# Weight conversion stores half a step earlier, a fourth float64 buffer, and 512-token x tiles in an attention and two-MoE kernel

## The chip, the cores and the metric

The kernel runs on one core of a Trainium2 chip. The metric is the device time of one execution in microseconds (us), lower is better; what is given for a kernel is the median of its runs.

## The reference

The input is attention over 4 batches of 8 heads, 576 positions, 64 dimensions per head, with a mask in blocks of 64, followed by two feed-forward layers ("MoE" in the names, with one expert each). All arithmetic is wanted at float32 accuracy; the weights arrive as float64.

```python
def _attn_ref(q, k, v):                       # 4 x 8 x 576 x 64
    scores = np.matmul(q, k.transpose(0, 1, 3, 2)) / np.sqrt(D)
    scores = np.where(pos[:, None] // 64 >= pos[None, :] // 64, scores, -1e9)
    attn = np.exp(scores - scores.max(-1, keepdims=True))
    attn = attn / (attn.sum(-1, keepdims=True) + 1e-09)
    return np.matmul(attn, v)

x = attn_out.transpose(0, 2, 1, 3).reshape(2304, 512)
h = x @ moe_w_in                              # 512 -> 2048
x = np.maximum(0.01 * h, h) @ moe_w_out       # 2048 -> 512
h = x @ moe2_w_in
P = a[0] + a[1] * h + a[2] * h**2 + a[3] * h**3
Q = 1.0 + abs(b[0]) * abs(h) + abs(b[1]) * h**2
out = (P / (Q + 1e-6)) @ moe2_w_out           # 2304 x 512
```

## The kernel before

Nearly every product is computed as three TensorE matmuls over a high and a low part of each operand (`xh`, `xl` for the attention output x; `wh`, `wl` for the weights). The program has three stretches.

**Attention** goes over 32 heads (`n`, batch `b = n // 8`). The steps of a head are letters in a string (`ORDER`): "1" splits q and k of the next head and loads a later one (L230, L231), "v" splits v and loads the next pair of heads, "x", "y", "z" are scores, maximum and exponential (L294, L300, L306), "a" and "b" the transposes and their split (L343, L328, L336), and "4" is `apply(n - 2)`, the product with v (`a4`, L371 and L375). At its end `a4` writes x. For the first eight heads ("whole") it is taken from PSUM by ACT and DVE (L382, L383). For the others ACT copies one half of the PSUM tile into `xs` (L385), DVE adds the other half (L386), and after every second head ACT and POOL split `xs`, which holds the 128 rows of two heads, into `xh` and `xl` (L388, L389). `xs` is part of the tile `vr`.

**The weight conversion** (`convert`, 64 blocks of 128x512 weights) runs between those steps. A block is loaded into `cs` as pairs of 32-bit words (L146, 512 KB). ACT changes the high word (L164), POOL (first 16 blocks) or ACT the low word (L168, L170), DVE joins the two into a float32 in `cl` (L179), ACT rounds its high part into `ch`, or for the first layer into the resident `w1i`, `w1o` (L182), and POOL subtracts it in place, which leaves the low part in `cl` (L183). The parts are stored to device memory by `write_block` (L153): 256 KB per block for the first 32 blocks (the low part only), twice 256 KB for the last 32, which are the second layer's weights. `cs` and `cl` have three buffers each, `ch` two. `convert` is a generator that yields twice per block. In the first half of a step it issues the load of block i+1 and the work of ACT and POOL on block i; in the second half the join, rounding and subtraction of block i-1, and then the stores of block i-2. A table of due times (`due`, `pace`) says how many halves have been issued after each attention step.

**The first feed-forward layer** (`moe1`) is the filler: from the second batch on `fill` puts some of its matmuls (L446) behind each attention step. Its work is cut into units of 12 matmuls, 32 units per batch of 512 tokens. A unit needs one tile of low weights, `wl`, which is read back from device memory (L418, 256 KB): `wl` has four buffers, and unit u, after its first matmul, issues the load for unit u+3. The 64 tokens per batch beyond 512 are stored to `xld` (`save_left`, L426, two stores of 128 KB per batch, of the high and the low part) and read back into the tile `xleft`, which makes a fifth group of 256 tokens and 32 units after the fourth batch. After the attention, `moe1` runs alone, and then **the second layer** (`moe2`, L548 to L602) follows.

The tiles `xh` and `xl` are 4x576 floats wide, of which `moe1` reads 4x512 directly.

What sets the order: the DMA queue of SP (every load and store of the kernel) is issued in the order of the program text, and SP waits at an instruction whose data or buffer is not ready. The instructions of the other engines are placed by a scheduler.

Of the kernel before, what the change touches and what calls it, by code (L numbers as in the profile page):

```python
# [25 lines left out]
def attention_moe_moe_kernel(  # L26
# [41 lines left out]
    xld = [dram.tile([P, KD, B, NL], F32, name=f"xld{i}") for i in range(2)]  # L68
# [34 lines left out]
    acc = w1.tile([P, KD, NT1], F32, name="acc")  # L103
    pTw = acc.rearrange("p k n -> p (k n)")
# [38 lines left out]
    def load_block(i):  # L143
        if i < len(blocks):
            stage[i] = cp.tile([P, 512, 2], I32, tag="cs", name="cs", bufs=3)
            nc.sync.dma_start(out=stage[i].rearrange("p (r n) w -> p r (n w)", r=KD), in_=blocks[i][0])  # L146
# [9 lines left out]
    def convert():  # L156
        load_block(0)
        load_block(1)
        for i in range(len(blocks) + 1):
            if i > 0:  # L160
                load_block(i + 1)
# [9 lines left out]
            if i > 0:  # L171
# [12 lines left out]
                write_block()  # L184
# [175 lines left out]
    def a4(n):  # L360
# [20 lines left out]
        if whole:  # L381
            nc.scalar.copy(xh[r, j, :], T[r, 384:960])  # L382
            nc.vector.tensor_tensor(xl[r, j, :], T[r, 384:960], xh[r, j, :].bitcast(F32), ALU.subtract)  # L383
# [3 lines left out]
        if e == 1:  # L387
            nc.scalar.copy(xh[:, j, :], xs)  # L388
            (nc.vector if h == H - 1 else nc.gpsimd).tensor_tensor(xl[:, j, :], xs, xh[:, j, :].bitcast(F32), ALU.subtract)  # L389

    X = {}

# [11 lines left out]
    wt = {}  # L404
    prepped = [0]

    def prep_w1(u):
        while prepped[0] <= min(u, len(units) - 1):
# [8 lines left out]
            wl = mp.tile([P, 4, P], F32R, tag="wl", name="wl", bufs=4)  # L417
# [5 lines left out]

    def save_left(b):
        for t, x in zip(xld, X[b]):
            nc.sync.dma_start(out=t[:, :, b, :], in_=x[:, :, NT1:S].bitcast(F32))  # L426

    def moe1(g):
        xh, xl = X[g]
        n = NT1 if g < B else B * NL  # L430
        for u in range(g * NU, (g + 1) * NU):
# [13 lines left out]
            for m, (w, kk, lo) in enumerate(seq):  # L445
                nc.tensor.matmul(T, lhsT=w[:, kk, :], rhs=A[kk][lo], start=(m == 0), stop=(m == 11))  # L446
                yield
                if m == 0:
                    prep_w1(u + 3)
# [56 lines left out]
    def x_tiles():  # L506
        return tuple(xp.tile([P, KD, S], F32R, tag=nm, name=nm) for nm in ("xh", "xl"))
# [128 lines left out]
    with tc.manual_schedule(engines={mybir.EngineType.SP}):  # L636
# [50 lines left out]
        for n, (b, h) in enumerate(heads):  # L687
# [8 lines left out]
            for step, f in zip(steps, fills):  # L696
# [9 lines left out]
                elif step == "4":  # L706
                    apply(n - 2)
# [20 lines left out]
            if h == 1 and b > 0:  # L728
                save_left(b - 1)
# [3 lines left out]
        apply(NHD - 1)  # L733
        att.close()
        xq.append(ctx.enter_context(tc.tile_pool(name="xq0", bufs=1, side="right", reuse_waits="tile")))
        w2a = ctx.enter_context(tc.tile_pool(name="w2a", bufs=1, side="right", reuse_waits="tile"))
        X[B] = tuple(w2a.tile([P, KD, B * NL], F32R, name=f"xleft{i}") for i in range(2))
# [3 lines left out]
        for i in range(32):  # L741
            fill(24)
            if i == 1:
                save_left(B - 1)
                for t, x in zip(X[B], xld):
                    nc.sync.dma_start(out=t.bitcast(F32), in_=x.rearrange("p k b t -> p k (b t)"))
# [53 lines left out]
```

## Time and profile before

| what | us |
|---|---|
| median of 3 runs | 1052.45 (1050.78 to 1053.03) |
| the profiled execution, its own time | 1051.65 |
| span of its trace | 1049.8 |
| TensorE matmul busy | 1001.1 (95%) |
| VectorE (DVE) busy | 725.7 (69%) |
| ScalarE (ACT) busy | 664.8 (63%) |
| GpSimd (POOL) busy | 297.4 (28%) |

The profile is of one execution. The difference between its time and the span, 1.85 us, lies outside the trace. The attention lasts to about 500 us (the last L385 starts at 499.4), the filler starts at about 85 us, the four full groups of the first layer end at about 597.8, the left-over group at about 646.6, and the second layer takes the rest. Engines are named as in the rows: PE is TensorE's matmuls, PEld its weight loads, SPq the queue on which SP issues DMAs. `L446 <- DVE vr L386` means that an instruction of line 446 waited for the DVE instruction of line 386 that writes `vr`.

### The profile page before, as it was taken

How to read it: one execution, taken by the hardware profiler on the slowest of the kernel's cores; microseconds unless marked ns; L12 is line 12 of the kernel's file. 1: busy time of each engine (PE TensorE's matmuls, PEld its weight loads, DVE VectorE, ACT ScalarE, POOL GpSimd, SP SyncE). 2: the span in 40 equal slices, each digit the busy share in tenths (PEclk: the TensorE clock that was granted, in tenths of full speed). 3: DMA queues.
4: the chain of work that ended last, by engine and by line, in shares of the span. 5: the costliest groups of instructions: out<-in, count | busy, mean ns of one | idle time of the engine just before them, and what ended most of it. 6: DMA issues, size and time to landing. Idle time of an engine off the chain costs nothing.

```text
span 1049.8 us, 14585 instructions
## 1 busy us (share of the span) xinstructions
PE 1001.1 (95%) x4968; PEld 826.8 (79%) x4968; DVE 725.7 (69%) x1232; ACT 664.8 (63%) x1355; POOL 297.4 (28%) x369
## 2 busy tenths in 40 slices
PE   6978888998999999999999999999999999999998
PEld 4757767777888878878888898888888888888886
DVE  3676767776667677775222223999888888888875
ACT  5766777867677776775311223876766666676675
POOL 4787646755454654543100101000000000000000
PEclk9999999999999999999999999999999999999999
DMA  7467768668666686564665588802102010110010
GB/s 195 148 179 244 223 203 269 204 211 275 202 190 210 220 275 196 190 211 121 226 205 197 188 278 295 327 1 81 41 1 81 1 40 1 41 41 1 1 41 21
DMA packets 104105, 159.36 MB, mean 152 GB/s; under 512 B 13152, under 2 KB 50016, under 8 KB 104032
## 3 DMA queue, kind: packets, MB, share of 16 engines
q1 hardware_dynamic: 104032, 158.44, 47.0%
q8 instruction: 39, 0.64, 0.3%
q14 instruction: 34, 0.28, 0.1%
HBM read 117.44 MB, written 40.37 MB: 150 GB/s over the span
## 4 chain that ended last, share of the span: by engine, by line
PE 60%; DMA 11%; DVE 9%; ACT 7%; POOL 6%; issue 4%; SPq 3%; POOLq 0%; DVEq 0%; ACTq 0%
PE h L548 19%; PE o L602 19%; PE M L446 18%; DMA cs<-in_moe_w_out_dram 4%; POOL PB L316 3%; DMA cs<-in_moe_w_in_dram 2%; ACT PB L306 2%; DVE cl L179 2%; PE T L343 1%; DVE pTl L336 1%; DMA w1l<-cl 1%; DVE nm L300 1%; DMA wl<-w1l 1%; POOL cl L183 1%; DMA w2l<-cl 1%
## 5 line engine op out<-in xcount | busy, mean ns | idle before, releaser
L446 PE MATMUL M<-gh,w1o 128*128 128x512 f32 (+1 forms) x320 | 120.3, 377 | 5.2 <-DVE vr L386 4.7
L446 PE MATMUL M<-gh,wl 128*128 128x512 f32 (+1 forms) x320 | 119.8, 375 | 0.3 <-DMA wl<-w1l 0.3
L446 PE MATMUL M<-gl,w1o 128*128 128x512 f32 (+1 forms) x320 | 120.0, 376 | 0.0
L316 POOL TENSOR_SCALAR PB<-PB,sm 128x448 f32<-128x448 f32 (+4 forms) x160 | 95.1, 616 | 65.4 <-DVE sm L313 61.4
L560 ACT ACTIVATE ea<-h,coef 128x512 f32<-128x512 f32 (+1 forms) x80 | 51.7, 646 | 93.5 <-PE h L548 93.5
L306 ACT ACTIVATE PB<-T,nm 128x448 f32<-128x448 f32 (+4 forms) x160 | 83.0, 524 | 35.7 <-DVE nm L300 29.0
L455 DVE TENSOR_TENSOR gl<-M,gh 128x512 fp32r<-128x512 f32 (+1 forms) x80 | 50.4, 633 | 79.1 <-ACT M L454 78.8
L453 ACT ACTIVATE gh<-M 128x512 fp32r<-128x512 f32 (+1 forms) x80 | 44.4, 555 | 93.4 <-PE M L446 93.2
L548 PE MATMUL h<-x2h,w2h 128*128 128x512 f32 (+1 forms) x240 | 89.0, 371 | 0.5 <-DVE acc L462 0.5
L548 PE MATMUL h<-x2h,w2l 128*128 128x512 f32 (+1 forms) x240 | 88.9, 370 | 0.0
L548 PE MATMUL h<-x2l,w2h 128*128 128x512 f32 (+1 forms) x240 | 88.8, 370 | 0.0
L602 PE MATMUL o<-w2h,g2l 128*128 128x512 f32 x216 | 84.7, 392 | 0.0
L602 PE MATMUL o<-w2h,g2h 128*128 128x512 f32 x216 | 84.7, 392 | 0.0
L602 PE MATMUL o<-w2l,g2h 128*128 128x512 f32 x216 | 84.6, 391 | 0.0
L343 PE MATMUL T<-ident,PB 128*128 128x128 f32 x480 | 68.9, 282 | 15.9 <-POOL PB L316 8.5
L300 DVE TENSOR_REDUCE nm<-T 128x1 f32<-128x448 f32 (+4 forms) x160 | 70.9, 479 | 15.6 <-PE T L288 9.9
L563 DVE SCALAR_TENSOR_TENSOR ea<-eh,coef,ea 128x512 f32<-128x512 f32 (+1 forms) x80 | 55.6, 696 | 35.7 <-ACT eh L561 35.2
L343 PEld LDWEIGHTS T<-ident,PB 128*128 128x128 f32 x480 | 56.2, 144 | 30.5 <-POOL PB L316 12.0
L179 DVE SCALAR_TENSOR_TENSOR cl<-cs 128x512 int32<-128x512 int32 x64 | 55.0, 859 | 36.4 <-DMA w2l<-cl 10.6
L446 PE MATMUL M<-xh,w1i 128*128 128x512 f32 x256 | 75.6, 404 | 3.8 <-DVE vr L386 3.2
L446 PE MATMUL M<-xh,wl 128*128 128x512 f32 x256 | 74.7, 408 | 0.0
L446 PE MATMUL M<-xl,w1i 128*128 128x512 f32 x256 | 72.6, 397 | 2.1 <-DVE xl L383 1.1
(117 smaller groups left out, 2504.3 us busy)
## 6 DMA issues: line engine op xcount, KB each, us to landing
wl<-w1l SPq DMA_DIRECT2D x160, 256.0 KB, 3.2
cs<-in_moe_w_in_dram SPq DMA_DIRECT2D x32, 512.0 KB, 5.0
cs<-in_moe_w_out_dram SPq DMA_DIRECT2D x32, 512.0 KB, 5.3
w1l<-cl SPq DMA_DIRECT2D x32, 256.0 KB, 4.7
w2h<-ch SPq DMA_DIRECT2D x32, 256.0 KB, 3.8
w2l<-cl SPq DMA_DIRECT2D x32, 256.0 KB, 3.9
w2h<-w2h SPq DMA_DIRECT2D x12, 512.0 KB, 7.0
w2l<-w2l SPq DMA_DIRECT2D x12, 512.0 KB, 7.7
```

Source lines behind the costliest of these rows:

```text
L179: nc.vector.scalar_tensor_tensor(f.bitcast(I32), hi, 3, lo, ALU.logical_shift_left, ALU.bitwise_or)
L300: nc.vector.tensor_reduce(nm[:, i:i + 1], sc, axis=AX.X, op=ALU.max, negate=True)
L306: nc.scalar.activation(PB[e][i][:, 0:ln], sc, AF.Exp, scale=SCALE if n == 0 else 1.0, bias=nm[:, i:i + 1], accum_out=sm[:, i:i + 1])
L316: nc.gpsimd.tensor_scalar(PB[e][i][:, 0:ln], PB[e][i][:, 0:ln], sm[:, i:i + 1], 1.0, ALU.mult, ALU.mult)
L343: nc.tensor.transpose(T[:, c:c + P], PB[e][i][:, kt * P:(kt + 1) * P], ident)
L446: nc.tensor.matmul(T, lhsT=w[:, kk, :], rhs=A[kk][lo], start=(m == 0), stop=(m == 11))
L453: nc.scalar.activation(gh, T, AF.Prelu, alpha=0.01)
L455: nc.vector.tensor_tensor(gl, T, gh.bitcast(F32), ALU.subtract)
L548: nc.tensor.matmul(h[:, 0:n], lhsT=a, rhs=x, start=(kk == 0 and i == 0), stop=(kk == KD - 1 and i == 2))
L560: nc.scalar.activation(a, h, AF.Abs, scale=coef[:, 4:5])
L563: nc.vector.scalar_tensor_tensor(a, h2, coef[:, 5:6], a, ALU.mult, ALU.add)
L602: nc.tensor.matmul(ob[t], lhsT=a, rhs=w, start=(f == 0 and i == 0), stop=(f == NF - 1 and i == 2))
```

## The change

**Conversion.** `cs` gets four buffers, and a step loads three blocks ahead (`load_block(i + 2)` where it was i+1). `write_block` is called right behind this load, at the top of the step's first half, instead of at the end of the second half: the same stores, half a step earlier in SP's order.

**x.** The tiles `xh`, `xl` are 4x512 wide. The left-over 64 tokens per batch are kept as float32: for the first batch, DVE copies them into a new tile `xf` (64x64 per head); for the others they are stored straight from `xs`. `save_left` is now called at step "4", ahead of `apply`, and stores what has been put on the list `left`: 32 KB per pair of heads (12 stores), and 128 KB once for the first batch. There is one `xld` of 512 KB instead of two, and one load of it into the low tile of `xleft`; then ACT rounds it into the high tile and POOL subtracts in place, three steps later (128x1024 each). ACT's copy into `xs` in the next even head's `a4` overwrites what the store reads, so it waits for this store.

**wl.** Three buffers instead of four, and unit u issues the load for u+2. From the sixth unit of the fourth batch on it is u+4, with two further buffers (`wl2`) in the memory that the attention has left.

```diff
--- before.py
+++ after.py
@@ -65,7 +65,7 @@
     NL = S - NT1
     x2hd = dram.tile([DM, NT], F32, name="x2hd")
     x2ld = dram.tile([DM, NT], F32, name="x2ld")
-    xld = [dram.tile([P, KD, B, NL], F32, name=f"xld{i}") for i in range(2)]
+    xld = dram.tile([P, KD, B, NL], F32, name="xld")
 
     att = ExitStack()
     ph1 = ExitStack()
@@ -101,6 +101,7 @@
     w1i = w1.tile([P, KD, DFF], F32R, name="w1i")
     w1o = w1.tile([P, NF, DM], F32R, name="w1o")
     acc = w1.tile([P, KD, NT1], F32, name="acc")
+    xf = w1.tile([P, KD, NL], F32, name="xf")
     pTw = acc.rearrange("p k n -> p (k n)")
 
 
@@ -142,7 +143,7 @@
 
     def load_block(i):
         if i < len(blocks):
-            stage[i] = cp.tile([P, 512, 2], I32, tag="cs", name="cs", bufs=3)
+            stage[i] = cp.tile([P, 512, 2], I32, tag="cs", name="cs", bufs=4)
             nc.sync.dma_start(out=stage[i].rearrange("p (r n) w -> p r (n w)", r=KD), in_=blocks[i][0])
 
     split = []
@@ -154,11 +155,12 @@
             ndone[0] += 1
 
     def convert():
-        load_block(0)
-        load_block(1)
+        for i in range(3):
+            load_block(i)
         for i in range(len(blocks) + 1):
             if i > 0:
-                load_block(i + 1)
+                load_block(i + 2)
+                write_block()
             if i < len(blocks):
                 hi, lo = stage[i][:, :, 1], stage[i][:, :, 0]
                 nc.scalar.activation(
@@ -181,7 +183,6 @@
                 )
                 nc.scalar.copy(wh, f)
                 nc.gpsimd.tensor_tensor(f.bitcast(F32R), f, wh.bitcast(F32), ALU.subtract)
-                write_block()
                 split.append(((dh, wh.bitcast(F32)), (dl, f))[kept:])
                 yield
         write_block()
@@ -379,16 +380,27 @@
         r = slice(e * 64, e * 64 + 64)
         xh, xl = X[b]
         if whole:
-            nc.scalar.copy(xh[r, j, :], T[r, 384:960])
-            nc.vector.tensor_tensor(xl[r, j, :], T[r, 384:960], xh[r, j, :].bitcast(F32), ALU.subtract)
+            nc.scalar.copy(xh[r, j, :], T[r, 384:384 + NT1])
+            nc.vector.tensor_tensor(xl[r, j, :], T[r, 384:384 + NT1], xh[r, j, :].bitcast(F32), ALU.subtract)
+            nc.vector.tensor_copy(xf[r, j, :], T[r, 384 + NT1:384 + S])
+            if h == H - 1:
+                left.append((xld[:, :, b, :], xf))
             return
         nc.scalar.copy(xs[r, :], T[64:128, 384:960])
         nc.vector.tensor_tensor(xs[r, :], T[0:64, 384:960], xs[r, :], ALU.add)
         if e == 1:
-            nc.scalar.copy(xh[:, j, :], xs)
-            (nc.vector if h == H - 1 else nc.gpsimd).tensor_tensor(xl[:, j, :], xs, xh[:, j, :].bitcast(F32), ALU.subtract)
+            x = xs[:, 0:NT1]
+            nc.scalar.copy(xh[:, j, :], x)
+            (nc.vector if h == H - 1 else nc.gpsimd).tensor_tensor(xl[:, j, :], x, xh[:, j, :].bitcast(F32), ALU.subtract)
+            left.append((xld[:, j, b, :], xs[:, NT1:S]))
 
     X = {}
+    left = []
+
+    def save_left():
+        while left:
+            dst, src = left.pop()
+            nc.sync.dma_start(out=dst, in_=src)
 
 
     NU = 2 * NF
@@ -402,6 +414,7 @@
             done = c
             units += [(g, "out", i, d) for d in range(KD)]
     wt = {}
+    wl2 = []
     prepped = [0]
 
     def prep_w1(u):
@@ -414,16 +427,15 @@
                 wh, src = w1i[:, :, i * P:(i + 1) * P], W1L[i]
             else:
                 wh, src = w1o[:, 4 * i:4 * i + 4, d * P:(d + 1) * P], W1L[NF + 4 * i + d]
-            wl = mp.tile([P, 4, P], F32R, tag="wl", name="wl", bufs=4)
+            if wl2 and w % 5 in (1, 3):
+                wl = wl2[0].tile([P, 4, P], F32R, tag="wl2", name="wl2", bufs=2)
+            else:
+                wl = mp.tile([P, 4, P], F32R, tag="wl", name="wl", bufs=3)
             nc.sync.dma_start(out=wl.bitcast(F32), in_=src)
             wt[w] = (wh, wl)
             prepped[0] += 1
 
     G = {}
-
-    def save_left(b):
-        for t, x in zip(xld, X[b]):
-            nc.sync.dma_start(out=t[:, :, b, :], in_=x[:, :, NT1:S].bitcast(F32))
 
     def moe1(g):
         xh, xl = X[g]
@@ -446,7 +458,7 @@
                 nc.tensor.matmul(T, lhsT=w[:, kk, :], rhs=A[kk][lo], start=(m == 0), stop=(m == 11))
                 yield
                 if m == 0:
-                    prep_w1(u + 3)
+                    prep_w1(u + (4 if u >= (B - 1) * NU + 5 else 2))
             if kind == "in":
                 gh = mp.tile([P, NT1], F32R, tag="gh", name="gh", bufs=5)[:, 0:n]
                 gl = mp.tile([P, NT1], F32R, tag="gl", name="gl", bufs=5)[:, 0:n]
@@ -504,7 +516,7 @@
         return pool.tile([P, 1024], F32R, name=f"w2h{f}"), pool.tile([P, 1024], F32R, name=f"w2l{f}")
 
     def x_tiles():
-        return tuple(xp.tile([P, KD, S], F32R, tag=nm, name=nm) for nm in ("xh", "xl"))
+        return tuple(xp.tile([P, KD, NT1], F32R, tag=nm, name=nm) for nm in ("xh", "xl"))
 
     def w2_in_x(pair, i):
         x = pair[i].rearrange("p k s -> p (k s)")
@@ -704,6 +716,7 @@
                     if odd and 0 < p < NHD // 2 - 1:
                         load_v(p + 1)
                 elif step == "4":
+                    save_left()
                     apply(n - 2)
                 elif step == "x":
                     a2_part(n, [(0, 4)], (nm, sm))
@@ -725,15 +738,16 @@
                 load_qk(NSF)
             if h == 0:
                 apply(n - 1)
-            if h == 1 and b > 0:
-                save_left(b - 1)
+        save_left()
         apply(NHD - 2)
         a3a(NHD - 1)
         a3b(NHD - 1)
         apply(NHD - 1)
+        save_left()
         att.close()
         xq.append(ctx.enter_context(tc.tile_pool(name="xq0", bufs=1, side="right", reuse_waits="tile")))
         w2a = ctx.enter_context(tc.tile_pool(name="w2a", bufs=1, side="right", reuse_waits="tile"))
+        wl2.append(w2a)
         X[B] = tuple(w2a.tile([P, KD, B * NL], F32R, name=f"xleft{i}") for i in range(2))
         pair = x_tiles()
         tiles = [w2_tiles(w2a, f) for f in range(NA)] + [w2_in_x(pair, f) for f in range(2)]
@@ -741,9 +755,10 @@
         for i in range(32):
             fill(24)
             if i == 1:
-                save_left(B - 1)
-                for t, x in zip(X[B], xld):
-                    nc.sync.dma_start(out=t.bitcast(F32), in_=x.rearrange("p k b t -> p k (b t)"))
+                nc.sync.dma_start(out=X[B][1].bitcast(F32), in_=xld.rearrange("p k b t -> p k (b t)"))
+            elif i == 4:
+                nc.scalar.copy(X[B][0], X[B][1].bitcast(F32))
+                nc.gpsimd.tensor_tensor(X[B][1], X[B][1].bitcast(F32), X[B][0].bitcast(F32), ALU.subtract)
             elif i < 14:
                 next(loads, None)
             elif i == 15:
```

How SP's order moves, at the place where the first pair of heads of the second batch has been written (rows of SP before; `cs<-` are loads of blocks, `w1l<-cl` stores of a block's low part, `wl<-` reads of low weights, `qk_` the q and k of a head):

```order
L153 DMA w1l<-cl 128x512
L230 DMA qk_87<-in_q_dram 64x576
L231 DMA qk_87<-in_k_dram 64x576
L418 DMA wl<-w1l 128x512
L146 DMA cs<-in_moe_w_out_dram 128x4x256
L153 DMA w1l<-cl 128x512
L146 DMA cs<-in_moe_w_out_dram 128x4x256
L418 DMA wl<-w1l 128x512 x2
L153 DMA w1l<-cl 128x512
```

The same place now:

```order
L231 DMA qk_86<-in_q_dram 64x576
L232 DMA qk_86<-in_k_dram 64x576
L403 DMA xld<-vr_88 128x64
L434 DMA wl<-w1l 128x512
L147 DMA cs<-in_moe_w_out_dram 128x4x256
L154 DMA w1l<-cl 128x512
L147 DMA cs<-in_moe_w_in_dram 128x4x256
L154 DMA w1l<-cl 128x512
L434 DMA wl<-w1l 128x512 x2
```

Every store of a block now stands directly behind the load of another one, where two `wl` reads stood between the last load and its store before; and the new store `xld<-vr` (`xs` lies in `vr`) stands behind the k load.

Later, where blocks of the second layer are converted (rows of SP before, around the loads of one head's q and k in the third batch):

```order
L230 DMA qk_87<-in_q_dram 64x576
L231 DMA qk_87<-in_k_dram 64x576
L146 DMA cs<-in_moe_w_in_dram 128x4x256
L418 DMA wl<-w1l 128x512
L153 DMA w2h<-ch 128x512
L153 DMA w2l<-cl 128x512
L418 DMA wl<-w1l 128x512 x2
L146 DMA cs<-in_moe_w_out_dram 128x1024
```

And now:

```order
L403 DMA xld<-vr_88 128x64
L434 DMA wl<-w1l 128x512
L231 DMA qk_86<-in_q_dram 64x576
L232 DMA qk_86<-in_k_dram 64x576
L147 DMA cs<-in_moe_w_out_dram 128x1024
L154 DMA w2h<-ch 128x512
L154 DMA w2l<-cl 128x512
L434 DMA wl<-w1l 128x512 x3
```

Load and stores of a block (1 MB) now follow one another without a `wl` read between them, and three `wl` reads stand behind them.

ACT around the copy into `xs` of the first pair's next head (before; `cs` are the conversion's first operations, `w1o<-cl` its rounding, `PB` the exponentials):

```order
L182 CAST w1o<-cl 128x4x128
L453 ACTIVATE gh<-M 128x512
L454 ACTIVATE M<-M 128x512
L182 CAST w1o<-cl 128x4x128
L385 COPY vr_89<-T 64x576
L272 CAST VHL_98<-vr_88 128x5x64
L164 ACTIVATE cs<-cs 128x512
```

And now:

```order
L184 CAST w1o<-cl 128x4x128
L465 ACTIVATE gh<-M 128x512
L466 ACTIVATE M<-M 128x512
L389 COPY vr_88<-T 64x576
L273 CAST VHL_97<-vr_87 128x5x64
L166 ACTIVATE cs<-cs 128x512
L172 ACTIVATE cs<-cs 128x512
```

The copy (L385, now L389) keeps its place behind the activations of the filler and ahead of the split of v; one rounding of the conversion that stood ahead of it no longer does.

## Rows read from the trace of the kernel before

**Rows 1.** Windows: stretch and length, busy us and instructions of each engine, clock, DMA share, GB/s.

```profile
85.00:500.00 415.00, 390.63 (x2024) 322.56 (x2024) 292.82 (x497) 294.13 (x641) 223.52 (x259) 0.99 0.68 214
500.00:597.80 97.80, 97.80 (x424) 79.28 (x423) 25.71 (x37) 22.45 (x41) 8.89 (x7) 1.00 0.61 202
597.80:646.60 48.80, 46.91 (x385) 45.86 (x383) 14.27 (x33) 12.40 (x36) 3.64 (x5) 1.00 0.85 281
```

**Rows 2.** Waits of PE, 85 to 500: us in total, times, longest us.

```profile
PE M L446 <- DVE vr L386: 7.8, 4, 3.0
PE T L294 <- DVE pTl L336: 5.8, 6, 2.4
PE T L343 <- ACT PB L306: 4.2, 7, 1.1
```

**Rows 3.** Waits of the other engines in the conversion, 85 to 500.

```profile
POOL cl L183 <- ACT ch L182: 54.1, 17, 7.9
...
ACT cs L164 <- DMA cs<-in_moe_w_in_dram: 16.5, 11, 3.6
ACT ch L182 <- DMA w2h<-ch: 15.1, 9, 3.4
ACT cs L164 <- DMA cs<-in_moe_w_out_dram: 12.8, 10, 3.6
...
DVE cl L179 <- DMA w2l<-cl: 10.6, 5, 3.5
...
DVE cl L179 <- DMA w1l<-cl: 7.6, 5, 2.1
```

**Rows 4.** Chain of waits, 85 to 500: its shares by line.

```profile
by line: PE M L446 13.1%; DMA cs<-in_moe_w_out_dram 9.3%; issue 8.9%; DMA cs<-in_moe_w_in_dram 5.5%; DVE cl L179 4.1%; ACT PB L306 3.7%; DVE pTl L336 3.4%; DMA w1l<-cl 3.2%; POOL PB L316 2.6%; DMA w2l<-cl 2.6%; POOL cl L183 2.6%; DVE nm L30
```

**Rows 5.** Timeline: start, us, engine and line, [idle before <-releaser].

```profile
109.94 0.69 DVE L179 SCALAR_TENSOR_TENSOR cl<-cs 128x512 int32<-128x512 int32 x1 [1.19 <-DMA w1l<-cl]
...
110.67 0.62 ACT L182 CAST w1o<-cl 128x512 fp32r<-128x512 f32 x1 [2.04 <-DVE cl L179]
111.31 0.64 ACT L385 COPY vr<-T 64x576 f32<-64x576 f32 x1
...
111.98 0.75 DVE L386 TENSOR_TENSOR vr<-T,vr 64x576 f32<-64x576 f32 x1 [1.34 <-ACT vr L385]
...
112.78 0.50 PE L446 MATMUL M<-gh,w1o 128*128 128x512 f32 x1 [3.01 <-DVE vr L386]
...
465.05 0.50 PE L446 MATMUL M<-gh,w1o 128*128 128x512 f32 x1 [1.64 <-DVE vr L386]
```

**Rows 6.** Groups by shape, 85 to 500: the conversion's first operation.

```profile
L164 ACT ACTIVATE cs<-cs 128x512 f32<-128x512 f32 x53 | 35.8, 678 | 29.4 <-DMA cs<-in_moe_w_in_dram 16.5 <-DMA cs<-in_moe_w_out_dram 12.8
```

**Rows 7.** Windows of line 446 alone: PE busy (x), PEld busy (x), clock, DMA share, GB/s.

```profile
85.00:500.00 415.00, 292.99 (x1115) 201.56 (x1116) 0.99 0.68 214
500.00:597.80 97.80, 97.80 (x424) 79.28 (x423) 1.00 0.61 202
```

**Rows 8.** DMA issues, whole run: count, KB each, median us to landing; then line 418's spread.

```profile
wl<-w1l SPq DMA_DIRECT2D x160, 256.0 KB, 3.2
...
vr<-in_v_dram SPq DMA_DIRECT2D x32, 32.0 KB, 2.8
...
xld<-xh SPq DMA_DIRECT2D x4, 128.0 KB, 4.8
...
DMA to landing us min/median/max: 2.5/3.2/6.9
```

**Rows 9.** Waits of PE, 597.8 to 646.6: us in total, times, longest.

```profile
PE M L446 <- DMA wl<-w1l: 1.1, 3, 0.4
```

**Rows 10.** Waits of SP's queue, 85 to 500.

```profile
SPq L153 <- POOL cl L183: 8.1, 4, 3.6
```

**Rows 11.** Timeline around one copy into xs.

```profile
143.21 0.48 SPq L231 DMA_DIRECT2D qk<-in_k_dram  x1
...
146.80 0.64 ACT L385 COPY vr<-T 64x576 f32<-64x576 f32 x1
```

## The prediction

> **What bounds the kernel now.** I read the windows of the page first, stage by stage. TensorE sets the end: from 85 to 500 us its matmuls are busy 390.63 of 415.00 us, from 500 to 597.8 all 97.80, from 597.8 to 646.6 46.91 of 48.80 [rows 1]. Since PE runs a fixed list of matmuls at a granted clock of 0.99 to 1.00 in these stages, the change can win only what PE idles there: 24.4 us in the attention stage and 1.9 us in the left-over stage. After 646.6 nothing of what the change touches is left.
>
> Next I asked what PE waits for in the attention stage. The top of the list is DVE and ACT results of the attention: 7.8 us for the sum into `xs` (L386), 5.8 us for the transposes' low part (L336), 4.2 us for exponentials (L306) [rows 2]. Nothing of the conversion shows there. But DVE is busy only 292.82 and ACT 294.13 of 415 us [rows 1], so neither is full, and the question is why they are late. The waits of these engines give the answer: ACT waits 16.5 and 12.8 us for loads of blocks and 15.1 us for a `w2h` store that still reads a `ch` buffer, DVE 10.6 and 7.6 us for stores that still read a `cl` buffer [rows 3], 62.6 us together. The chain of waits says the same by another road: loads of blocks are 9.3 and 5.5% of it, stores of `w1l` and `w2l` 3.2 and 2.6%, more than any attention operation [rows 4]. What sits behind such a wait on its engine is delayed with it. The timeline shows one case whole: at 109.94 DVE's join had waited 1.19 us for a `w1l` store; ACT's rounding follows at 110.67, then, on ACT, the copy into `xs` at 111.31, DVE's sum at 111.98, and PE starts at 112.78 after 3.01 us idle [rows 5].
>
> I followed each idle stretch of PE over 0.1 us back in this way. There are 30 of them, 24.3 us in all. 27 of them, 22.5 us, end at one of 15 such DMA waits; the first is the 3.01 us at 112.78, the last the 1.64 us at 465.05 [rows 5].
>
> **The change part by part.**
>
> *Loads and stores sooner.* 53 blocks begin in these 415 us [rows 6], 7.8 us per block, so half a step is 3.9 us. Stores gain half a step, loads a whole one (three blocks ahead instead of two). The longest waits for them are 3.6 us for a load, 3.4 and 3.5 us for a store [rows 3], all shorter than what is gained, so if SP issues at its new place, the 62.6 us go. What is PE's share? The upper end is all of its idle time, 24.4 us. The lower end is nothing (rival A), and below nothing if the new order delays something else (rival B). Between: a wait cannot cause more idle time than it lasts, so I counted for each of the 15 the smaller of its length and the gaps behind it: 13.9 us. A second measure is coarse: ACT and DVE idle 120.9 + 122.2 = 243.1 us [rows 1], of which 62.6 are these waits, 26%; 26% of PE's 24.4 us are 6.3 us. The true value should lie between, nearer the traced one, as that follows instructions and the other only averages; but engines that arrive earlier will meet other waits. I take **-10 us**.
>
> *Low weights two units ahead instead of three.* 1115 filler matmuls in 415 us are 93 units of 12, 4.5 us per unit; where the filler runs alone, 424 matmuls take 97.80 us, 2.77 us per unit [rows 7]. A read of `wl` lands in 3.2 us, 6.9 at most [rows 8]. Two units are about 9 us on average and 5.5 us where they stand back to back, so the median read is still covered and the slowest are not. I moved the issue of about 100 reads of the trace by one unit each: with the landings as they are, 3 come too late, by **+1.7 us** together. With every landing 1.4 us later it would be 9 us, with 2 us later 16.5, with 3 us later 30; nothing at the other end.
>
> *Four units ahead at the end.* From the sixth unit of the last batch the lead grows. The left-over group's units are half as long, and there PE waits 1.1 us for `wl` [rows 9] of 1.9 us idle [rows 1]: **-1.5 us**, between 0 and -1.9.
>
> *x.* The split of `xs` shrinks by 64 of 576 columns on ACT and POOL or DVE. DVE gets 8 copies of 64x64 for the first batch; its sum of 64x576 takes 0.75 us [rows 5], so they are below 6 us together and by width about 0.7; DVE has slack for them, and without it they cost that 0.7. SP loses 8 stores of 128 KB and a 512 KB load and gets 12 stores of 32 KB and one of 128. At the end ACT and POOL split 128x1024 once, where they are busy 22.45 and 8.89 of 97.80 us [rows 1] and the left-over group is still far off: nothing; if that cover were gone, a few operations of some 0.6 to 3 us. Together **+0.3 us**.
>
> *A new wait.* ACT's copy into `xs` (L385 before) must now wait for the store of `xs` of the pair before. Behind it on ACT are the split of v and the conversion's first operations, and DVE's sum waits for it. The store is issued right behind a k load or a `wl` read. In the row pair for the second batch the k load is issued at 143.21 and the copy starts at 146.80 [rows 11], so a store issued at about 143.7 has 3.1 us. The nearest rows for its landing: 2.8 us for 32 KB reads of v, 4.8 us for 128 KB stores of the left-over tokens [rows 8]. With the first it costs nothing here, with the second 1.7 us; over ten such copies, not all alike, I make it 2 us of ACT time to 12. I take the small end, since 32 KB is nearer, and ACT's slack covers it: 0 in the sum; the other end is rival C.
>
> The sum is -10 + 1.7 - 1.5 + 0.3 = **-9.5 us**. The profiled execution took 1051.65 us, so it would take about 1042.2; the median of the runs is 0.8 us above it, so I forecast **1043.0** for the median.
>
> **The rivals.** A measurement of this kernel can tell 0.2%, 2.1 us, from no change.
>
> A, *the waits move.* Taking the DMA waits away lets ACT and DVE reach the next thing sooner, and that is often each other: POOL already waits 54.1 us for ACT's `ch` [rows 3], PE for DVE and ACT results that would be as late if those engines are simply given conversion work in clumps. SP may not reach the new place in time either: it issues in order, and a store half a step sooner finds POOL's subtraction unfinished. Now it waits 8.1 us for that, four times, 3.6 at the longest [rows 10]. For: PE's list names only ACT and DVE. Against: the traced chains end at DMA waits. It gives 1051 to 1053, no change.
>
> B, *the shorter lead of `wl` bites*, and this one ends slower. Before, stores and `wl` reads were mixed; now a load and two stores, 1 MB, stand together ahead of three `wl` reads, and whenever SP waits for POOL at a store, those reads wait too. The DMA engines are 0.68 busy [rows 1], so a read can queue. It decides when reads land about 1.4 us later than now, which makes 9 us and eats the gain; at 2 us later, 16.5 us, the kernel takes 1043.0 - 1.7 + 16.5 = 1058. For: the slowest read takes 6.9 us already [rows 8]. Against: half of them land in 3.2 us, and the average lead is 9.
>
> C, *the copy into `xs` waits for its store*, 12 us on ACT, at a point where PE already waits most (L386, 7.8 us [rows 2]). If all of it reaches PE, the gain of 9.5 is turned into 2.5 us lost, 1055. The row shows that such stores are slow for their size: 128 KB in 4.8 us, while a `wl` read of 256 KB takes 3.2 [rows 8]. The Trainium skill, DMA: Bandwidth & Descriptors, Specifications, asks for transfers of at least 512 B for line rate and says that smaller ones are read, modified and written; a piece of these stores is 64 floats, 256 B. By that rule the new stores keep the slow rate and C is the likelier end; the trace agrees as far as that row goes, but they have a quarter of the bytes, so I leave the chance small.
>
> **How the numbers follow.** The forecast's mechanism, with a gain above 2.1 us, gets 0.72; its own range is 1036 (16.5 us gained: most of the traced 13.9 and more of the 24.4) to 1050. A gets 0.12, B 0.11, C 0.05. So faster 0.72, same 0.12, slower 0.16. The range goes from 1036 to 1054: it takes in the forecast's range and A, and leaves out B, most of C and the few cases below.
>
> **What would show it.** If right, in the attention stage: PE idle falls from 24.4 to about 14 us; the five waits of 62.6 us on DMA fall to under 15; PE's 7.8 us for L386 shrinks by half; the left-over stage loses its waits for `wl`. A would show the DMA waits gone and PE's idle time unchanged. B would show PE waiting for `wl` in the attention stage, where it does not now. C would show ACT waiting for `xld` at the copy into `xs`. The forecast is wrong if the DMA waits remain, or if they go and PE's end does not move.

## The result and the profile after

The change made the kernel slower: 1060.26 us, median of 5 runs (1057.25 to 1062.05), against 1053.03 (1050.78 to 1056.47), a ratio of 1.0059 with a 95% interval of 1.0032 to 1.0086. Timed again beside other kernels (e5 below) it was 1.0066 (1.0041 to 1.0091). The forecast was 1043.0, faster, in a range that ended at 1054. Ratios are of executions in the fast state alone: one slow execution of e6 (1395.83 us), which the median of e6 still counts, and one of the kernel before beside e5 to e8 (1635.22) are left out of them.

The profiled execution of the changed kernel took 1062.05 us, its span is 1060.2, 10.4 more than before. Line numbers have moved: L164 to L172 are now L166 to L172, the join is L181, the rounding L184, the subtraction L185, the stores L154, the copy into `xs` L389, the filler L458. The last copy into `xs` starts at 509.3 us instead of 499.4, so nearly all of the 10.4 us arises in the attention. The windows, cut at the new ends of the stages (columns as in [rows 1]):

```profile
85.00:510.00 425.00, 396.05 (x2024) 326.98 (x2024) 288.62 (x498) 292.60 (x638) 224.32 (x259) 0.98 0.66 206
510.00:608.30 98.30, 97.97 (x423) 79.13 (x423) 25.56 (x37) 23.43 (x41) 11.31 (x8) 1.00 0.60 199
608.30:657.00 48.70, 46.24 (x385) 45.55 (x383) 14.29 (x33) 12.41 (x36) 3.59 (x5) 1.00 0.81 275
```

The first row has the same 2024 matmuls as the first of [rows 1]. PE idles 29.0 us instead of 24.4 and is busy 396.05 us with them instead of 390.63, at a granted clock of 0.98 instead of 0.99: 4.6 us of more waiting and 5.4 us of slower matmuls. This execution is the slowest of the five; in the profile of e5, the same kernel (1057.80 us), the last copy starts at 506.4, and the 7.0 us up to there are 3.7 of waiting and 3.3 of slower matmuls. The other two stages are within 0.5 us of what they were.

The waits of the conversion, 85 to 510, have not gone. To compare with [rows 3]:

```profile
POOL cl L185 <- ACT ch L184: 92.5, 18, 10.4
...
DVE cl L181 <- DMA w2l<-cl: 29.7, 14, 5.1
ACT cs L166 <- DMA cs<-in_moe_w_out_dram: 28.0, 16, 4.4
...
ACT cs L166 <- DMA cs<-in_moe_w_in_dram: 15.5, 10, 3.6
...
DVE cl L181 <- DMA w1l<-cl: 5.9, 3, 2.2
...
ACT ch L184 <- DMA w2h<-ch: 2.7, 5, 1.2
...
ACT vr L389 <- DMA xld<-vr: 0.3, 1, 0.3
```

The five waits that were 62.6 us are now 81.8. Loads three blocks ahead are waited for longer (43.5 us, it was 29.3); of the stores `w2h` and `w1l` are waited for less, `w2l` much more. ACT's waits for loads and `w2h` together are 46.2 us, 44.4 before; DVE's for stores are 35.6, 18.2 before. The last row is the new wait of the change, 0.3 us, once. What PE and SP wait for in this stretch (answers to [rows 2] and [rows 10]):

```profile
PE T L344 <- ACT PB L307: 7.9, 9, 2.3
PE M L458 <- DVE vr L390: 6.3, 5, 2.2
PE M L458 <- ACT PB L307: 4.7, 1, 4.7
PE M L458 <- DMA wl<-w1l: 3.7, 3, 2.4
```

```profile
SPq L434 <- PE M L458: 137.0, 54, 7.6
...
SPq L154 <- POOL cl L185: 18.6, 6, 7.1
```

SP's longest stands are at reads of `wl`, until PE has freed a buffer: 137.0 us, where it was 147.4 (85 to 500). It stands 18.6 us at a store until POOL has subtracted; it was 8.1. PE waits 3.7 us for low weights, for which it did not wait in this stage before. The longest idle time of PE, 4.7 us, shows how these go together (timeline, columns as in [rows 5]):

```profile
176.42 0.41 SPq L147 DMA_DIRECT2D cs<-in_moe_w_in_dram  x1
...
184.00 0.32 SPq L154 DMA_DIRECT2D w1l<-cl  x1
...
186.12 1.11 DVE L181 SCALAR_TENSOR_TENSOR cl<-cs 128x512 int32<-128x512 int32 x1 [1.79 <-DMA w1l<-cl]
...
187.15 1.67 DVE L301 TENSOR_REDUCE nm<-T 128x1 f32<-128x576 f32 x3
...
188.27 0.73 ACT L307 ACTIVATE PB<-T,nm 128x576 f32<-128x576 f32 x1
...
189.15 0.79 PE L458 MATMUL M<-gh,w1o 128*128 128x512 f32 x1 [4.71 <-ACT PB L307]
```

After a load SP comes to the store at 176.8 and stands there until 184.0: POOL was at the attention's normalisation (L317, 3.55 us from 178.72) and then had three subtractions in a row (4.43 us from 182.24). DVE's join at 186.12 has waited for just this store to free its `cl` buffer, and the attention's row maxima (L301), the exponential and PE come behind it. In DVE's order before the change the same join (the 32nd) stood behind these row maxima:

```
before: L273 TENSOR_TENSOR VHL_98<-vr_88,VHL_98 128x5x64
        L300 TENSOR_REDUCE nm<-T 128x1 x3
        L179 SCALAR_TENSOR_TENSOR cl<-cs 128x512
now:    L274 TENSOR_TENSOR VHL_97<-vr_87,VHL_97 128x5x64
        L181 SCALAR_TENSOR_TENSOR cl<-cs 128x512
        L301 TENSOR_REDUCE nm<-T 128x1 x3
```

The scheduler has put it ahead of them. Its move is no single case. For blocks 17 to 64 I counted how many of the attention's exponentials (ACT) or row maxima (DVE) stand ahead of each operation in the two programs: ACT's first operation stands 2.2 exponentials earlier, the rounding 0.9, DVE's join 1.1 row maxima earlier. There are five per head, and a head takes 16.9 us (24 copies into `xs`, from 111.3 to 499.4), so that is some 7.4, 3.2 and 3.7 us: what the prediction had counted as the lead of loads (7.8) and stores (3.9). SP itself does issue earlier: placed by their times in the traces between the exponentials in the same way (blocks 17 to 60), the loads go out 2.2 exponentials earlier than before and the stores 0.9. The order hands the lead to the operations that use the data, and they meet the DMA where they met it before. The stores of the second layer's weights land later, too (before, then now; median over the run, us):

```profile
w2h<-ch SPq DMA_DIRECT2D x32, 256.0 KB, 3.8
w2l<-cl SPq DMA_DIRECT2D x32, 256.0 KB, 3.9
```

```profile
w2h<-ch SPq DMA_DIRECT2D x32, 256.0 KB, 5.0
w2l<-cl SPq DMA_DIRECT2D x32, 256.0 KB, 5.1
```

SP's stand for POOL is not where most of the time is lost. Its six stands lie between 103 and 184 us. The ninth copy into `xs` starts at 260.7 us, 2.4 later than before (258.3); the last one is 9.9 later, so 7.5 us arise behind the ninth (5.4 of 7.0 in e5). From 250 us on SP waits for POOL's subtraction nowhere, PE idles 13.9 us instead of 8.1, and DVE waits 25.5 us for `w2l` (before, then now; windows, the later one with 11 matmuls more, then DVE's wait):

```profile
250.00:500.00 250.00, 241.89 (x1273) 202.90 (x1272) 174.59 (x304) 174.12 (x383) 126.11 (x151) 0.99 0.65 206
250.00:510.00 260.00, 246.11 (x1284) 204.89 (x1283) 173.40 (x307) 173.48 (x384) 128.01 (x151) 0.99 0.63 197
```

```profile
DVE cl L179 <- DMA w2l<-cl: 9.6, 4, 3.5
DVE cl L181 <- DMA w2l<-cl: 25.5, 12, 5.1
```

The clock behind the idle stretch at 184 us (windows of PE: busy, clock, DMA share, GB/s):

```profile
184.00:187.00 3.00, 0.43 (x3) 1.00 0.57 176
187.00:189.00 2.00, 0.00 (x0) 0.76 1.03 207
189.00:190.00 1.00, 0.85 (x2) 0.50 0.86 272
190.00:192.00 2.00, 2.00 (x6) 0.50 0.88 338
192.00:194.00 2.00, 2.00 (x9) 0.50 0.02 6
194.00:196.00 2.00, 2.00 (x10) 0.78 0.00 0
```

PE did almost nothing from 184 to 189; the granted clock fell to 0.50, the lower level of 1.2 GHz, and stayed there for some 5 us of full work.

### The profile page after: what moved, and what is told of

It is laid out like the page before. It is cut to its first block, busy times and chain, and to the rows that moved or that the text cites. A ratio compares the mean times of both kernels' runs of the same rounds, so it can differ in the third digit from the quotient of the medians.

```text
span 1060.2 us, 14579 instructions
## 1 busy us (share of the span) xinstructions
PE 1009.0 (95%) x4968; PEld 832.2 (78%) x4968; DVE 722.4 (68%) x1240; ACT 664.9 (63%) x1356; POOL 302.4 (29%) x370
## 3 DMA queue, kind: packets, MB, share of 16 engines
q1 hardware_dynamic: 101920, 157.39, 46.2%
## 4 chain that ended last, share of the span: by engine, by line
PE 63%; DMA 11%; DVE 8%; ACT 5%; POOL 4%; issue 4%; SPq 4%; DVEq 0%; POOLq 0%; ACTq 0%
PE M L458 20%; PE h L560 19%; PE o L614 19%; DMA cs<-in_moe_w_out_dram 3%; PE T L344 3%; DMA wl<-w1l 2%; DMA w1l<-cl 2%; POOL PB L317 2%; PE T L376 2%; ACT PB L307 1%; DMA w2l<-cl 1%; DVE nm L301 1%; DVE cl L181 1%; DMA w2h<-ch 1%; POOL cl L185 1%
## 5 line engine op out<-in xcount | busy, mean ns | idle before, releaser
L458 PE MATMUL M<-gh,w1o 128*128 128x512 f32 (+1 forms) x320 | 121.7, 380 | 5.2 <-ACT PB L307 4.7
L458 PE MATMUL M<-gh,wl 128*128 128x512 f32 (+1 forms) x320 | 121.3, 379 | 2.9 <-DMA wl<-w1l 2.9
L458 PE MATMUL M<-gl,w1o 128*128 128x512 f32 (+1 forms) x320 | 121.1, 378 | 0.0
L317 POOL TENSOR_SCALAR PB<-PB,sm 128x448 f32<-128x448 f32 (+4 forms) x160 | 96.4, 621 | 54.2 <-DVE sm L314 51.2
L344 PE MATMUL T<-ident,PB 128*128 128x128 f32 x480 | 71.9, 289 | 15.5 <-ACT PB L307 7.9
L181 DVE SCALAR_TENSOR_TENSOR cl<-cs 128x512 int32<-128x512 int32 x64 | 55.5, 868 | 45.1 <-DMA w2l<-cl 29.7
L458 PE MATMUL M<-xh,w1i 128*128 128x512 f32 x256 | 77.1, 410 | 6.7 <-DVE vr L390 5.8
L301 DVE TENSOR_REDUCE nm<-T 128x1 f32<-128x448 f32 (+4 forms) x160 | 71.2, 480 | 17.6 <-PE T L289 9.9
L344 PEld LDWEIGHTS T<-ident,PB 128*128 128x128 f32 x480 | 58.5, 148 | 29.8 <-POOL PB L317 11.9
L458 PE MATMUL M<-xh,wl 128*128 128x512 f32 x256 | 73.8, 404 | 3.2 <-DMA wl<-w1l 3.1
L458 PEld LDWEIGHTS M<-gh,w1o 128*128 128x128 f32 x320 | 61.1, 191 | 15.6 <-ACT PB L307 5.0
```

Of the source, the lines that this page charges most:

```text
L181: nc.vector.scalar_tensor_tensor(f.bitcast(I32), hi, 3, lo, ALU.logical_shift_left, ALU.bitwise_or)
L301: nc.vector.tensor_reduce(nm[:, i:i + 1], sc, axis=AX.X, op=ALU.max, negate=True)
L317: nc.gpsimd.tensor_scalar(PB[e][i][:, 0:ln], PB[e][i][:, 0:ln], sm[:, i:i + 1], 1.0, ALU.mult, ALU.mult)
L344: nc.tensor.transpose(T[:, c:c + P], PB[e][i][:, kt * P:(kt + 1) * P], ident)
```

## The experiments

Theories, as the expectations name them. **C**: the scheduler's move of the consumers, and SP's stand at the stores, cost the time. **W**: the shorter lead of the low weights does. **X**: the handling of the left-over tokens does. **I**: the loss needs both the loads and stores that C finds crowded together and W's shorter lead. **F** and **G** (last round): the loss comes from the earlier stores (F) or from the first operations standing earlier (G). "Held" means that an instruction may not be issued ahead of the one before it in the program on its engine:

```diff
+    pin = tc.keep_in_program_order
...
-                nc.scalar.activation(hi.bitcast(F32), ...
+                pin(nc.scalar.activation(hi.bitcast(F32), ...
```

**e1, conversion undone**, in the changed kernel:

```diff
-  ... name="cs", bufs=4)
+  ... name="cs", bufs=3)
...
-                load_block(i + 2)
-                write_block()
+                load_block(i + 1)
...
+                write_block()
                 split.append(...)
```

> The changed kernel with the conversion as it was: three buffers for float64 blocks, loads two blocks ahead, stores at the end of the second half. Theory C (the scheduler moves the conversion's first operations and its join forward by as much as loads and stores were moved, so ACT and DVE still run into the DMA, and SP is held at stores): 1053 to 1056 us. Theory W (the shorter lead of the low weights costs the time): 1059 to 1061, nothing won back. Theory X (the new handling of the left-over tokens costs it): 1059 to 1061.

Measured: 1054.03 us, ratio 1.0016 (0.9991 to 1.0040). As C: without the conversion's part there is no loss.

**e2, x alone**: as e1, and

```diff
-  ... name="wl", bufs=3)
+  ... name="wl", bufs=4)
...
-                    prep_w1(u + (4 if u >= (B - 1) * NU + 5 else 2))
+                    prep_w1(u + 3)
```

> As the first, and the low weights as before too (four buffers, three units ahead, no further buffers at the end): only the 512-token x tiles and the float32 left-over are left of the change. Theory C: 1052 to 1054. Theory W: 1052 to 1054, some 7 us under the first run. Theory X: 1058 to 1061.

Measured: 1054.02, 1.0015 (0.9997 to 1.0033). X falls, and without the conversion's change the shorter lead of `wl` costs nothing: e1 and e2 are equal.

**e3, four wl buffers** in the changed kernel (`u + 2` becomes `u + 3`, the end stays):

> The changed kernel with four wl buffers and three units of lead in the attention as before; the further buffers at the end stay; the first batch's left-over tile lies in an unused part of acc, to make room. Theory C: 1056 to 1059, the 4 us of PE waiting for wl won back. Theory W: 1052 to 1054. Theory X: 1059 to 1061.

Measured: 1054.43, 1.0026 (1.0000 to 1.0052). Some 4 us under the changed kernel in e5, though the intervals overlap. That is W's figure, where e1 had C's: each undoing alone takes most of the loss away, so neither theory holds by itself, and theory I was formed for the next round.

**e4, two operations held**: ACT's first operation and DVE's join.

> The changed kernel, but ACT's first operation and DVE's join of each block may not be issued ahead of the instruction that stands before them in the program on their engine. By the order of instructions, the first operations stand 1.3 exponentials earlier than before the change instead of 2.2, the roundings 1.6 later instead of 0.9 earlier. Theory C: ACT's waits for loads fall from 43.5 us to under 20, DVE's for stores from 35.6 to under 10, and the time falls to 1052 to 1057. Theories W and X: 1059 to 1061 whatever these waits do.

Measured: 1055.36, 1.0019 (0.9999 to 1.0038). DVE's waits for stores went, ACT's for loads did not: its second operation on a block, which was not held, floated ahead of the first and waited 41.2 us for the loads in its place. (In the trace the held first operations stand 0.8 exponentials later than before the change, not 1.3 earlier as I had counted; the second ones stand 2.3 earlier.) For ACT's part it is a half-made test. Yet some 0.5% of the loss is gone (e5), with ACT still waiting for loads and with SP standing 47.5 us at stores for POOL.

**e5, the change again**, on one chip with e6 to e8:

> The changed kernel as it is, timed beside the next three on one chip. The first timing was 5 runs (1060.3 us), the experiments of the first round had 12. If the first figure holds: 1058 to 1061. If the change is nearer to the four variants than it looked: 1054 to 1057.

Measured: 1058.47, 1.0066 (1.0041 to 1.0091). The loss holds.

**e6, three operations held** (both first ones and the join), else the changed kernel:

> As e4, and ACT's second operation of a block (the low word) is held in program order too: in e4 it had floated ahead of the first and waited for the load in its place. Theory C (moving loads forward is spent by the scheduler): ACT's waits for loads fall from 43 us to under 10, DVE's for stores stay near 0, PE's idle time in the attention stage falls by 5 us or more, 1046 to 1052 us. Theory I (the loss needs both the clumped loads and stores and the shorter lead of wl; the waits of ACT and DVE are not what PE waits for): waits fall, the time stays at 1053 to 1056.

Measured: 1042.44, 0.9898 (0.9872 to 0.9925). C's direction, and more than its range; I falls. PE idles 20.6 us from 85 us to the last copy into `xs` (24.4 before, 29.0 in the change), though SP stands 47.5 us at the stores for POOL: that stand alone does not cost the time. Held, the operations do not stand where they stood before the change but later: the first ones by 0.8 exponentials, the roundings by 1.6, the joins by 2.9 row maxima. What is left of ACT's and DVE's waits for loads and stores of blocks, 85 to 500:

```profile
ACT ch L185 <- DMA w2h<-ch: 3.6, 1, 3.6
...
ACT cs L167 <- DMA cs<-in_moe_w_in_dram: 3.1, 1, 3.1
```

**e7, the same with four wl buffers**:

> As e6 with four wl buffers and three units of lead in the attention. Theory C: another 2 to 4 us under e6, 1043 to 1050. Theory I: with one half of the loss already away, within 2 us of e6.

Measured: 1041.78, 0.9903 (0.9876 to 0.9930), as e6. The 2 to 4 us that C expected did not come (this point is I's); once the operations are held, no cost of the shorter lead of `wl` can be told.

**e8, the kernel before with the three operations held**:

> The kernel before with the same three operations held in program order, nothing else changed: they then stand 1.1 exponentials later on ACT, the roundings 1.6 later. If the order alone is what helps e6: as fast as e6. Theory C: holding them gives the loads their lead even with two blocks, so ACT's waits for loads fall under 15 us and the time to 1048 to 1052; if the later rounding costs more, 1053 to 1057.

Measured: 1051.72, 0.9990 (0.9974 to 1.0006). ACT's waits for loads fell from 29.3 to 13.8 us, all five waits of the prediction from 62.6 to 16.1, and nothing was won: PE idles 25.4 us up to the last copy, 24.4 before (waits of ACT, then of SP's queue, 85 to 500):

```profile
ACT cs L165 <- DMA cs<-in_moe_w_in_dram: 8.2, 4, 2.5
...
ACT cs L165 <- DMA cs<-in_moe_w_out_dram: 5.6, 5, 1.7
```

```profile
SPq L146 <- DVE cl L180: 33.7, 16, 4.0
```

With the join later and three buffers, SP waits for a free `cs` buffer: 33.7 us, where it was 2.7. So the order alone is not what helps e6, and a shorter sum of these waits is not yet time.

**e9, e10, e11**: e6 with only the loads moved (stores back at the end of the second half), with only the stores moved (three buffers, two blocks ahead), and with neither.

> e6 with the stores back at the end of the second half: of the conversion's change only the fourth buffer and the loads three blocks ahead are left, with the three operations held in program order. If the loads carry the gain: 1042 to 1045, and DVE's and ACT's waits for stores come back to 10 us or more without cost. If the stores carry it: 1050 to 1053. If each has a part: about 1047.

> e6 with three buffers and loads two blocks ahead: of the conversion's change only the earlier stores are left, with the three operations held. If the stores carry the gain: 1042 to 1045; if the loads do: 1050 to 1053, with 10 to 15 us of ACT's waits for loads as in e8.

> e6 without any of the conversion's change, so the x tiles and the low weights of the change with the three operations held. Theory C: as e8, 1050 to 1053, since neither loads nor stores have more lead. If the gain of e6 comes from the x tiles, the tail or the order: 1042 to 1045.

Measured: 1040.44, 0.9871 (0.9840 to 0.9902); 1057.73, 1.0047 (1.0020 to 1.0073); 1054.23, 1.0007 (0.9986 to 1.0028). I had allowed for a gain from loads, from stores or from both; that the stores would lose was in none of the three, and all three times lie outside the ranges I gave. The loads win some 14 us (e11 to e9) or 15 (e10 to e6). The stores lose some 3.5 us from e11 to e10; from e9 to e6 it is 0.3%, which is within the noise. In e10 SP stands 49.6 us at the stores (30.0 in e11), and PE waits for `wl` 3.8 us (1.7).

**e12, e13**: the same split without holding anything. e12 is the changed kernel with its stores back, e13 with its loads back.

> The changed kernel with the stores back at the end of the second half, nothing held in program order. By the order of instructions the first operations stand 2.1 exponentials earlier than before, the roundings where they were. Theory F (the first operations' move forward spends the loads' lead, and that alone loses nothing; the loss comes from the earlier stores): 1052 to 1055. Theory G (the loss comes from the first operations standing earlier): 1057 to 1060.

> The changed kernel with three buffers and loads two blocks ahead, stores early, nothing held. The first operations stand where they did before, the roundings 0.8 earlier. Theory F: 1056 to 1060. Theory G: 1052 to 1055.

Measured: e12 1048.22, 0.9973 (0.9952 to 0.9994); e13 1060.75, 1.0086 (1.0065 to 1.0107). F's direction, though e12 is some 4 us under F's range and e13 0.75 over it: with the first operations 2.1 exponentials earlier e12 still wins, so G falls. The joins and roundings move with the stores, though (1.1 row maxima and 0.8 exponentials earlier in e13), so with nothing held the earlier stores and the earlier joins are not told apart; held, where the joins stay, the loss is 0.4% (e11 to e10) instead of 0.7 (e1 to e13). e13 against e1, which has the stores late (waits, 85 to 500, e13, then e1):

```profile
ACT cs L166 <- DMA cs<-in_moe_w_in_dram: 27.5, 13, 4.0
...
DVE cl L181 <- DMA w2l<-cl: 18.2, 8, 4.4
...
ACT cs L166 <- DMA cs<-in_moe_w_out_dram: 14.5, 11, 3.0
...
ACT ch L184 <- DMA w2h<-ch: 1.3, 3, 0.8
```

```profile
ACT ch L183 <- DMA w2h<-ch: 15.1, 9, 3.9
ACT cs L165 <- DMA cs<-in_moe_w_out_dram: 14.1, 12, 3.0
...
DVE cl L180 <- DMA w2l<-cl: 12.0, 5, 3.0
...
ACT cs L165 <- DMA cs<-in_moe_w_in_dram: 11.6, 9, 3.0
```

ACT waits 42.0 us for loads instead of 25.7, though by the count above they are issued at the same place (within 0.2 exponentials) and land as fast (median of blocks 17 to 60: 4.7 us, 4.8 in e1). What ACT no longer waits for is `w2h`, 1.3 us instead of 15.1. Its waits for loads and `w2h` together are 43.3 us, 40.8 in e1: most of the waiting has only moved from a store to a load. DVE's waits for `w2l` rise from 12.0 to 18.2, and PE's for `wl` from 1.6 to 3.6. SP stands 10.5 us at stores for POOL, 4.5 in e1. Which of these make the 7 us is not shown.

**e14, the best of the parts**: loads three blocks ahead, stores late, three operations held, four `wl` buffers.

> e9 (loads three blocks ahead, stores late, three operations held) with four wl buffers and three units of lead in the attention: 1038 to 1041 if the waits of PE for wl that e9 keeps are worth their 2 us; as e9, 1040 to 1041, if not.

Measured: 1039.61, 0.9879 (0.9859 to 0.9898), as e9. It beats both kernels. From 85 to 500 us PE is busy 398.78 us and does 43 matmuls more than in [rows 1], and of ACT's waits for loads 1.8 us are left:

```profile
85.00:500.00 415.00, 398.78 (x2067) 0.98 0.69 219
```

```profile
ACT cs L166 <- DMA cs<-in_moe_w_in_dram: 1.1, 1, 1.1
...
ACT cs L166 <- DMA cs<-in_moe_w_out_dram: 0.7, 2, 0.4
```

The conversion's parts in one table, ratio to the kernel before:

| loads, stores | not held | three operations held |
|---|---|---|
| two ahead, late | 1.0016 (e1) | 1.0007 (e11) |
| three ahead, late | 0.9973 (e12) | 0.9871 (e9) |
| two ahead, early | 1.0086 (e13) | 1.0047 (e10) |
| three ahead, early | 1.0066 (e5, the change) | 0.9898 (e6) |

## Why the prediction was wrong

The step that failed is in the first part of the sum, "Loads and stores sooner": "if SP issues at its new place, the 62.6 us go", which gave -10 us.

- **The step itself.** Its condition held on average: SP issues the loads some 7.4 us earlier in the attention's course and the stores some 3.0. What does not follow is that the waits go. I took ACT's and DVE's operations as staying in place; the scheduler moved them forward by as much, and the waits are 81.8 us.
- **Stores.** I counted their move as lead won. Moved alone it loses in all four pairs of the table: 0.7 and 0.9% with nothing held, 0.4 and 0.3% held, the last within the noise. In the change itself, undoing it alone turns 1.0066 into 0.9973 (e12). `w2l` lands 1.2 us later while the join that needs its buffer comes as much earlier as the store goes out, and DVE's waits for stores double, from 18.2 to 35.6 us. ACT's waits for `w2h` go (15.1 to 2.7), but it then waits for loads: in every run with nothing held the two together are between 40.6 and 46.9 us. That is rival A's "the waits move", at a loss and not at its "no change". How a loss of 0.7 to 0.9% comes of these is in part argued. The stand at POOL that rival A named is 18.6 us instead of 8.1 and shows in the idle stretch at 184 us, but no such stand lies behind 250 us, where most of the time is lost, and e6 has 47.5 us of it and wins.
- **From waits to idle time.** The -10 us also took it that PE's idle time follows the five waits. It does not by their sum: e12 and e13 have 63.1 and 62.9 us of them, as the kernel before (62.6), at 0.9973 and 1.0086; e8 has 16.1 and wins nothing. And the sum had no term for the clock, which is 5.4 of the 10.0 us lost in the attention of this profile.
- **Loads.** A gain of the size that I forecast is there once the operations are held: 0.9898 with the whole change (e6), 1042.4 us against my 1043.0. That the figure is so near is luck: in the forecast loads and stores both won, in e6 the loads win some 15 us and the stores add nothing, and the held operations stand later than before. Holding alone wins nothing (e8, e11). Not held, the loads are worth 0.4% (e12 against e1; e13 to e5, 0.2%, is within the noise), held 1.4% (e9 against e11). I had printed ACT's order at one copy into `xs` and looked at what the change moved there, not at where the conversion's operations stood against the attention's over all blocks; that count was to be had before the run.
- **Low weights, +1.7 us.** Three reads came too late, as counted, but by 3.7 us, and e3 gives back about 4 us. Without the conversion's change (e1 against e2), or with the operations held (e6 against e7, e9 against e14), no cost of the shorter lead can be told. Rival B (chance 0.11) had its sign, PE waiting for `wl`, and nearly the time (1058), but the time by luck: it needed reads that land 2 us later and 16.5 us of waiting; they land in 3.2 us as before (median), and PE waits 3.7 us in the attention, 2.4 in e5.
- **The end, -1.5 us.** Not seen: the left-over stage took 48.7 us and had 2.46 us of PE idle. PE still waits 2.0 us for `wl` there. In e14, with four buffers, the left-over group takes 46.7 us (587.0 to 633.7, before 48.8); in e11, with three, it takes as long as before. So the sign is open.
- **x, +0.3 us, and the new wait, 0.** Right within what can be told: e2 is 1.0015 with 1 in its interval; ACT waits 0.3 us for the store, once (5.5 us in four waits in e6, which is faster all the same). Rival C falls: the 32 KB stores land in 2.4 us (median; 1.8 to 6.3) and the 128 KB store of the first batch in 2.3, where 128 KB took 4.8 [rows 8]. So the rule that I cited from the Trainium skill, DMA: Bandwidth & Descriptors, Specifications, did not by itself set the time of pieces of 256 B here; the measurement decides.

What stays open: e8 and e11 take about half of ACT's waits for loads away and nearly all of those for stores, and win nothing, while e9 takes nearly all of both and wins 14 us. Part of the waiting had gone over to SP in e8 (33.7 us for a `cs` buffer), but e9 has 23.5 us of that too. Nor is it shown why e12 wins 0.4% over e1 with equal waits for loads (27.2 and 25.7 us). And no run held the operations exactly where they stood before the change.

## What to carry to other kernels

Where one queue's order is written by hand and a scheduler places the other engines, moving a transfer earlier can move its consumers as well: count where they stand, before pricing the lead, and hold them in program order if the lead is to stay. A sum of waits is not a price: a wait that is taken away can come back at the next thing the engine needs, as ACT's for `w2h` did at the loads. Undo each half of such a change alone: here one half won up to 15 us with the order held, and the other lost up to 10 with the order free.

## What the runs showed of the hardware

A store that is issued directly behind a 512 KB load lands later: `w2h` 3.7 us and `w2l` 3.9 with the stores at the end of the half-step (e1), 4.9 and 5.1 directly behind the load (e13); held, 4.1 and 3.7 (e11) become 4.9 and 4.9 (e10). The 512 KB loads themselves land no later (4.8 us in e1, 4.7 in e13, medians of blocks 17 to 60). And a stretch of 5 us in which PE was nearly idle was followed by some 5 us of work at the lower clock, which is paid beside the wait itself: of the 10 us lost in the attention stage, 5.4 are longer matmuls at the lower mean clock and 4.6 are idle time (3.3 and 3.7 of 7.0 in e5).
